# Load order, early weight conversion and early products in an attention + gated MLP + SoLU MLP kernel

## The chip, the cores and the metric

One NeuronCore of a Trainium2 chip runs the whole program. The metric is the device time of one execution in microseconds (us); lower is better. Engines are named as in the profile: PE (TensorE matmul), PEld (its weight loads), DVE (VectorE), ACT (ScalarE), POOL (GpSimd), SP (SyncE, which here only issues DMAs).

## The reference

```python
def _attn_ref(q, k, v):                    # 2 x 12 heads, 448 x 64, fp32, causal
    scores = scale * np.matmul(q, k.transpose(0, 1, 3, 2))
    scores = np.where(mask, -1000000000.0, scores)
    scores = scores - np.max(scores, axis=-1, keepdims=True)
    attn = np.exp(scores)
    attn = attn / (np.sum(attn, axis=-1, keepdims=True) + 1e-09)
    return np.matmul(attn, v)

def _moe_ref(x, w_gate, w_val, w_out):     # x 896 x 768, w_gate/w_val 768 x 1536, w_out 1536 x 768
    gate = 1.0 / (1.0 + np.exp(-(x @ w_gate)))
    return gate * (x @ w_val) @ w_out

def _moe2_ref(x, w_in, w_out, g_ln):       # w_in 768 x 1024, w_out 1024 x 768
    h = x @ w_in
    solu = h * softmax(h)
    ln = (solu - mu) / np.sqrt(var + 1e-06) * g_ln
    return ln @ w_out
```

The attention output, heads side by side, is the `x` of the first MLP, whose output is the `x` of the second. The weights arrive as 64-bit floats, given to the kernel as pairs of 32-bit words, and are turned into fp32 on the chip.

## The kernel before, in words

**Stages.** The attention works on 12 pairs of heads (`NPR`), pair 0 to 5 being batch 0 and 6 to 11 batch 1. Then come the gate/value products (L564, weight chunks 0 to 23), the product with `w_out` (L594), the product with `w_in` with the SoLU and normalisation (L626), and the last product (L687). Everything after the attention is one long row of matmuls, fed by weight chunks of 128 x 768 that pass through small rings of buffers.

**One pair of heads.** PE makes the scores (`sc_mm`, L299 and L309, tile `s`), DVE takes their row maxima (`sc_max`, L324), ACT the exponentials with their row sums (`sc_exp`, L336, tile `p`), PE transposes the exponentials in four parts u = 0 to 3 (`tr_mm`, L381, tile `t`, a ring of three PSUM buffers), which DVE (u = 0, 1; L392) and ACT (u = 2, 3; L390) copy to SBUF (tile `pt`), and PE multiplies them with v (`pv_mm`, L404, tile `x`, one PSUM buffer). The row sums go a way of their own: POOL adds a small number (`sums`, L340), DVE takes reciprocals and transposes them (`recips`, L344, L345, tile `rs32q`), SP writes them to DRAM in four small DMAs (`rs_rows`, L350, tile `rd`) and reads them back spread over 64 partitions each in two (`rs_bcast`, L356, tile `rb`). DVE then multiplies `x` by `rb` (`x_mul`, L410, tile `xf`), ACT rounds the product to the matmul type (`x_hi`, L414), and POOL subtracts that from it (`x_lo`, L419): `xy` holds a high and a low part, and each product is three matmuls. POOL also scales q (`prep_q`, L226) when `load_qk` (L218, 448 KB a pair, a ring of three) has brought it; `load_v` (L223, 256 KB) brings v.

**What sets the order.** The program has a manual schedule: each engine executes in the order in which the code issues to it, and a wait holds up all that stands behind it on that engine. `STEPS` lists, for each action, the step it belongs to within a pair; a pair begins every `PER` = 8 steps, so that action `s0` of pair p is issued at step 8p + s0, engine letter by engine letter within a step (E, A, D, S, P). SP is one such queue: the loads, the small writes and the reads of the reciprocals stand in one line.

**Weight chunks.** A chunk of 64-bit words is brought to a `raw` buffer (two of them), and `bits_steps` makes fp32 of it: ACT scales (L118), DVE does three bit operations (L121, L123, L126, tile `t`), and after the last one the load of the next chunk is issued (`dma_next`, L106). `chunk_hi` (ACT, L137) and `chunk_lo` (DVE, L140) make the high and low parts (tile `hl`). Chunks 0 and 1 are loaded in parts during the attention (`FIRST_RAW`, L99). Before, their conversion is issued at steps 86 to 103, that is with pairs 10 and 11 on the way, and that of chunks 2 and 3 at steps 102 to 117.

**Early products.** Of the first gate/value tile, the half of batch 0 needs only pairs 0 to 5, so its 36 matmuls (`early_tiles`, L436, tile `gv`) are dealt out among the last pairs' work, as soon as `hl` of chunks 0 and 1 is there: before, from step 96 on, up to two a step, the rest after the last step.

```python
        for s in range(PER * NPR + 26):
            steps(s, 'E')
            for _ in range(2):
                if s >= PER * NPR and left and next(early):
                    left -= 1
```

When a group of 18 is complete, ACT copies it to SBUF (tile `pre`, L441), in the place of its queue where the last matmul was issued. Two short matmuls (L181) stand between the last early product and the first one of L564.

Of the kernel before, what the change touches and what calls it, by code (L numbers as in the profile page):

```python
# [15 lines left out]
ALU = mybir.AluOpType  # L16
# [22 lines left out]
def f32(ap):  # L39
    return ap.bitcast(F32)  # L40
# [3 lines left out]
def attn_moe_moe2(ctx: ExitStack, tc: tile.TileContext, qk, v, w_gv, w_out, w_in2, w_out2, g_ln, out):  # L44
# [3 lines left out]
    nc = tc.nc  # L48
# [84 lines left out]
        for _ in bits_steps(it):  # L133
            pass

    def w_hi(it, hi):
        nc.scalar.copy(out=hi, in_=t_t[it])  # L137

    def w_lo(it, hi, lo):
        nc.vector.tensor_tensor(out=lo, in0=t_t.pop(it), in1=f32(hi), op=ALU.subtract)  # L140

    def chunk_hi(c):
        if c < NCH and c not in hl_t:
            hl_t[c] = ring.tile([128, 2, CH], FR, tag="hl", name="hl")
# [55 lines left out]
    with ExitStack() as actx:  # L200
# [242 lines left out]

        NPR = NH // 2
        PER = 8
        FIRST_RAW = {34: (0, 0, 1), 42: (0, 1, 2), 50: (0, 2, 3), 58: (0, 3, 4),
                     66: (1, 0, 1), 74: (1, 1, 3), 82: (1, 3, 4)}
        early = early_tiles()
        left = NE * 6 * NK

        STEPS = (
            (0, 'E', lambda p: sc_mm(p, (0, 1)), 3), (2, 'E', lambda p: sc_mm(p, (1,)), 2, 3),
            *((9 + 2 * u, 'E', lambda p, u=u: tr_mm(p, u), int(u < 2)) for u in range(4)),
            (17, 'E', lambda p: pv_mm(p, 0, 1)), (18, 'E', lambda p: pv_mm(p, 3, 2)),
            (16, 'A', lambda p: tr_copy(p, 3, 'A')),
            (1, 'A', lambda p: sc_exp(p, (3,)), 2), (2, 'A', lambda p: sc_exp(p, (0,)), 2),
            (5, 'A', lambda p: sc_exp(p, (2,)), 1), (6, 'A', lambda p: sc_exp(p, (1,)), 1),
            (23, 'A', x_hi), (15, 'A', lambda p: tr_copy(p, 2, 'A')),
            (8, 'D', recips), (-1, 'D', lambda p: sc_max(p, 3, 0), 2, 3), (0, 'D', lambda p: sc_max(p, 3, 0), 3),
            (2, 'D', lambda p: sc_max(p, 2), 2), (3, 'D', lambda p: sc_max(p, 1), 2),  # L460
            (12, 'D', lambda p: tr_copy(p, 0, 'D'), 1), (21, 'D', x_mul), (14, 'D', lambda p: tr_copy(p, 1, 'D'), 1),
            (7, 'P', sums, 1), (-8, 'P', prep_q, 3), (24, 'P', x_lo),
            (8, 'S', rs_rows), (8, 'S', rs_bcast), (-2, 'S', lambda p: load_qk(p + 2), 1), (11, 'S', lambda p: load_v(p + 2)),
        )

        sc_mm(0, (0, 1))
# [28 lines left out]
                    f(p)  # L495


        for s in range(PER * NPR + 26):
            steps(s, 'E')
            for _ in range(2):  # L500
                if s >= PER * NPR and left and next(early):
                    left -= 1
            steps(s, 'A')
            steps(s, 'D')
            steps(s, 'S')
            steps(s, 'P')
# [3 lines left out]
            for c in range(2 * NE + 2):  # L510
                e = s - 86 - 8 * c
                if e in (3, 5, 7):
                    next(bits_now)
                if e == 8 and c < 2 * NE:
                    chunk_hi(c)
                if e == 9 and c < 2 * NE:
                    chunk_lo(c)
                if e == 0:
                    bits_now = bits_steps(c)
                    next(bits_now)  # L520
# [237 lines left out]
```

## Time and profile before

| | |
|---|---|
| median of 3 runs | 488.84 us (486.95 to 490.61) |
| the profiled execution | 489.1 us, of which its span is 487.3 |
| PE busy | 476.5 us (98%), 2727 matmuls |
| DVE / ACT / POOL busy | 305.1 / 207.6 / 72.0 us |
| mean granted TensorE clock | 0.993 |
| DMA | 55.56 MB, mean 114 GB/s |

Busy times come from one profiled execution. Its time is that of the whole execution; the span runs from its first to its last instruction, and the 1.8 us between them are not in the trace. Matmuls are pipelined, so the duration of one overlaps the next; what a row of them costs is read from the chain of waits, where each piece is counted once. All times in the sections below are counted from the start of the span.

### The profile page before, as it was taken

The page shows a single profiled execution, that of the slowest core. Times are in us where ns is not written, and L with a number is a line of the kernel's source. Part 1 is how long each engine was busy: PE and PEld are TensorE (multiplying, and loading weights), DVE is VectorE, ACT ScalarE, POOL GpSimd, SP SyncE. Part 2 cuts the span into 40 slices and gives each one's busy share as a digit, 9 for nine tenths or more (in the row PEclk, how much of TensorE's full clock was granted, in tenths as well). Part 3 has the DMA queues.
Part 4 walks back from the last instruction along what each step waited for, and adds up shares of the span by engine and source line. Part 5 has one row for each costly group of instructions (what it writes and reads, how often), then busy time and mean ns, then how long its engine had stood idle before and what let it go on. Part 6 is the DMA issues. An engine that isn't in the chain of part 4 may idle for free.

```text
span 487.3 us, 7096 instructions
## 1 busy us (share of the span) xinstructions
PE 476.5 (98%) x2727; PEld 412.7 (85%) x2727; DVE 305.1 (63%) x472; ACT 207.6 (43%) x441; POOL 72.0 (15%) x121
## 2 busy tenths in 40 slices
PE   9999987899999999999999999999999999999997
PEld 7666654579999999999999999999988888899997
DVE  5676666765676777887777666777726978811110
ACT  4787768453235345345344233243321524232111
POOL 2222212110000000000000000000151778510000
PEclk9999999799999999999999999999999999999999
DMA  5245353342234335454335225444322130001001
GB/s 195 81 159 164 124 189 132 134 164 65 82 114 150 112 126 174 139 164 147 118 124 195 90 84 172 136 164 142 119 108 66 65 101 30 1 32 66 32 34 65
DMA packets 16401, 55.56 MB, mean 114 GB/s; under 512 B 2800, under 2 KB 5616, under 8 KB 16368
## 3 DMA queue, kind: packets, MB, share of 16 engines
q1 hardware_dynamic: 16368, 55.11, 33.7%
q8 instruction: 21, 0.34, 0.3%
q14 instruction: 12, 0.10, 0.1%
HBM read 52.30 MB, written 2.80 MB: 113 GB/s over the span
## 4 chain that ended last, share of the span: by engine, by line
PE 87%; DMA 5%; SPq 3%; DVE 2%; ACT 1%; issue 1%; POOL 0%; DVEq 0%; ACTq 0%; POOLq 0%
PE gv L564 34%; PE pm L594 18%; PE po L687 12%; PE h L626 12%; DMA rd<-rs32q 3%; PE x L404 2%; PE gv L436 2%; PE s L309 2%; PE t L381 2%; DMA rb<-rd 1%; PE tp L669 1%; ACT p L336 1%; SPq L350 1%; DVE sum L324 1%; SPq L356 1%
## 5 line engine op out<-in xcount | busy, mean ns | idle before, releaser
L564 PE MATMUL gv<-xy,hl 128*128 128x448 f32 x828 | 168.1, 365 | 0.0
L564 PEld LDWEIGHTS gv<-xy,hl 128*128 128x128 f32 x828 | 155.4, 188 | 12.3
L594 PE MATMUL pm<-g,hl 128*128 128x448 f32 x432 | 87.7, 365 | 0.0
L594 PEld LDWEIGHTS pm<-g,hl 128*128 128x128 f32 x432 | 81.1, 188 | 6.4
L687 PE MATMUL po<-wo,lt 128*128 128x384 f32 x336 | 60.7, 340 | 0.0
L140 DVE TENSOR_TENSOR hl<-t,hl 128x768 fp32r<-128x768 f32 x36 | 34.5, 958 | 40.9 <-ACT hl L137 39.2
L626 PE MATMUL h<-wi,xy 128*128 128x512 f32 x252 | 59.3, 396 | 0.0
L687 PEld LDWEIGHTS po<-wo,lt 128*128 128x128 f32 x336 | 58.7, 188 | 0.2 <-POOL wo L616 0.2
L626 PEld LDWEIGHTS h<-wi,xy 128*128 128x128 f32 x252 | 47.1, 188 | 11.4
L123 DVE SCALAR_TENSOR_TENSOR t<-raw,t 128x768 int32<-128x768 int32 (+1 forms) x56 | 54.3, 969 | 1.9
L118 ACT ACTIVATE raw<-raw 128x768 f32<-128x768 f32 (+1 forms) x56 | 48.0, 866 | 9.9 <-DMA raw<-in_wo_dram 6.1
L126 DVE SCALAR_TENSOR_TENSOR t<-raw,t 128x768 int32<-128x768 int32 (+1 forms) x56 | 51.2, 913 | 1.6
L336 ACT ACTIVATE p<-s,sum 128x320 f32<-128x320 f32 (+3 forms) x92 | 42.2, 484 | 10.1 <-DVE sum L324 8.1
L611 POOL TENSOR_SCALAR t<-t,g_sb 128x768 f32<-128x768 f32 x8 | 9.0, 1121 | 247.9 <-PE pm L594 247.9
L137 ACT CAST hl<-t 128x768 fp32r<-128x768 f32 x36 | 30.0, 832 | 11.9 <-DVE t L126 7.7
L121 DVE TENSOR_SCALAR t<-raw 128x768 int32<-128x768 int32 (+1 forms) x56 | 31.2, 557 | 2.8 <-ACT raw L118 2.8
L177 DVE TENSOR_TENSOR lt<-tp,lt 128x512 fp32r<-128x512 f32 x14 | 9.7, 690 | 36.4 <-ACT lt L176 36.4
L404 PE MATMUL x<-pt,vr 128*64 128x384 f32 (+3 forms) x168 | 30.5, 425 | 0.0
L189 ACT ACTIVATE wk<-gv 128x448 f32<-128x448 f32 x23 | 11.3, 542 | 44.2 <-PE gv L564 44.2
L324 DVE TENSOR_REDUCE sum<-s 128x2 f32<-128x640 f32 (+3 forms) x44 | 27.4, 677 | 3.5 <-PE s L309 3.5
L309 PE MATMUL s<-qkr,qs 64*128 64x448 f32 (+3 forms) x192 | 28.0, 416 | 0.0
L381 PE MATMUL t<-ident,p 128*128 128x128 f32 x180 | 25.3, 279 | 1.3 <-DVE pt L392 0.9
(90 smaller groups left out, 388.6 us busy)
## 6 DMA issues: line engine op xcount, KB each, us to landing
raw<-in_gv_dram SPq DMA_DIRECT2D x22, 768.0 KB
raw<-in_wo_dram SPq DMA_DIRECT2D x20, 768.0 KB
raw<-in_wi_dram SPq DMA_DIRECT2D x12, 512.0 KB
qkr<-in_qk_dram SPq DMA_DIRECT2D x11, 448.0 KB
vr<-in_v_dram SPq DMA_DIRECT2D x12, 256.0 KB
rb<-rd SPq DMA_DIRECT2D x24, 112.0 KB
out_dram<-o SPq DMA_DIRECT2D x6, 384.0 KB
raw<-in_gv_dram SPq DMA_DIRECT2D x6, 192.0 KB
```

The source lines that it names most:

```text
L118: nc.scalar.activation(out=w1.bitcast(F32), in_=w1.bitcast(F32), func=AF.Copy, scale=2.0 ** -112)
L123: nc.vector.scalar_tensor_tensor(out=tt, in0=w1, scalar=-2 ** 31, in1=tt, op0=ALU.bitwise_and, op1=ALU.bitwise_or)
L126: nc.vector.scalar_tensor_tensor(out=tt, in0=w0, scalar=29, in1=tt, op0=ALU.logical_shift_right, op1=ALU.bitwise_or)
L140: nc.vector.tensor_tensor(out=lo, in0=t_t.pop(it), in1=f32(hi), op=ALU.subtract)
L309: nc.tensor.matmul(out=ps_sc[p, i][1 - e], lhsT=q_sc[p % 2][rows, n - D:n + D], rhs=k[rows, S - n:] if e else k[rows, :n], start=False, st ...
L336: nc.scalar.activation(out=p_t[p % 2][:, POFF[i] + (1 - e) * n:POFF[i] + (2 - e) * n], in_=ps_sc[p, i][1 - e], func=AF.Exp, bias=mx, scale ...
L381: nc.tensor.transpose(ps[:, max(c, 0):max(c, 0) + 128], p_t[p % 2][:, k:k + 128], ident if c >= 0 else identx)
L404: nc.tensor.matmul(out=ps_pv[pr][d, q0:], lhsT=v_raw[pr % 3][:, (j - 1) % NQ, d], rhs=pt_t[pr][:, u, c0:c0 + S - q0], start=(j == 0), stop ...
L564: nc.tensor.matmul(out=ps[i, b], lhsT=w[:, a, cs], rhs=xy[kk][:, x, b * S:(b + 1) * S], start=(kk == 0 and a == 0 and x == 0), stop=(kk == ...
L594: nc.tensor.matmul(out=ps[b], lhsT=w[:, a, cs], rhs=g_t[kk][:, x, b * S:(b + 1) * S], start=(kk == 0 and a == 0 and x == 0), stop=(kk == N ...
L626: nc.tensor.matmul(out=h[:, n * 512:(n + 1) * 512], lhsT=xy[kk][:, a, tk], rhs=wi[n * NK + kk][:, c], start=(kk == 0 and i == 0), stop=(kk ...
L687: nc.tensor.matmul(out=ps[n], lhsT=lts[k // 4][:, a, k % 4], rhs=wo[k][:, c, cs], start=(k == 0 and i == 0), stop=(k == NF2 - 1 and i == 2))
```

## The change

The change has four parts.

**SP's order.** `load_qk(p + 2)` is issued at step 8p instead of 8p - 2, and `rs_bcast` at step 8p + 10 instead of 8p + 8. With `FIRST_RAW` at steps 9, 17, ... 65 (eight quarters of 192 KB, instead of seven loads at steps 34 to 82), the loads of q and k and of a quarter chunk now stand between the writes and the reads of one pair's reciprocals.

**Conversion of chunks 0 and 1.** Its steps are issued by a table (`FIRST_BITS`): chunk 0 at steps 64 (ACT), 68 (two DVE steps) and 76 (the third, and the load of chunk 2), chunk 1 at 72, 76 and 84 (and the load of chunk 3). The high and low parts are made by POOL instead of ACT and DVE, at steps 77 and 79, 85 and 87. Chunks 2 and 3 follow at steps 96 to 109.

**Early products.** `EARLY` deals 2, 3, 3, 3 and 10 of them at steps 96, 97, 99, 101 and 103; the other 15 follow after the last step. The first two blocks of pair 10's `pv_mm` are issued at step 98 instead of 97, beside the other two.

**Pair 0.** Its copies u = 2 and u = 3 of the transposed exponentials go from ACT to DVE.

```diff
-    def w_hi(it, hi):
-        nc.scalar.copy(out=hi, in_=t_t[it])
+    def w_hi(it, hi, eng='A'):
+        if eng == 'A':
+            nc.scalar.copy(out=hi, in_=t_t[it])
+        else:
+            nc.gpsimd.tensor_scalar(out=hi, in0=t_t[it], scalar1=1.0, scalar2=1.0, op0=ALU.mult, op1=ALU.mult)
...
+    def w_lo(it, hi, lo, eng=nc.vector):
+        eng.tensor_tensor(out=lo, in0=t_t.pop(it), in1=f32(hi), op=ALU.subtract)
...
-        FIRST_RAW = {34: (0, 0, 1), 42: (0, 1, 2), 50: (0, 2, 3), 58: (0, 3, 4),
-                     66: (1, 0, 1), 74: (1, 1, 3), 82: (1, 3, 4)}
+        FIRST_RAW = {9 + 8 * n: (n // 4, n % 4, n % 4 + 1) for n in range(8)}
+        FIRST_BITS = {64: (0,), 68: (0, 0), 76: (0, 1), 72: (1,), 84: (1, 1),
...
+        FIRST_HI, FIRST_LO = {77: 0, 85: 1}, {79: 0, 87: 1}
+        EARLY = {96: 2, 97: 3, 99: 3, 101: 3, 103: 10}
...
-            (17, 'E', lambda p: pv_mm(p, 0, 1)), (18, 'E', lambda p: pv_mm(p, 3, 2)),
-            (16, 'A', lambda p: tr_copy(p, 3, 'A')),
+            (17, 'E', lambda p: pv_mm(p, 0, 1), 0, NPR - 2), (18, 'E', lambda p: pv_mm(p, 0, 1), NPR - 2, NPR - 1),
+            (17, 'E', lambda p: pv_mm(p, 0, 1), NPR - 1), (18, 'E', lambda p: pv_mm(p, 3, 2)),
+            (16, 'A', lambda p: tr_copy(p, 3, 'A'), 1), (16, 'D', lambda p: tr_copy(p, 3, 'D'), 0, 1),
...
-            (8, 'S', rs_rows), (8, 'S', rs_bcast), (-2, 'S', lambda p: load_qk(p + 2), 1), (11, 'S', lambda p: load_v(p + 2)),
+            (8, 'S', rs_rows), (0, 'S', lambda p: load_qk(p + 2), 1), (10, 'S', rs_bcast), (11, 'S', lambda p: load_v(p + 2)),
```

On SP, around the reciprocals of pair 4, the queue before reads so (`rd` is the writes, `rb` the reads, `qkr` and `vr` the loads of a later pair, `raw` a part of a chunk):

```order
L350 DMA rd_641<-rs32q0_149 8x32 x4
L356 DMA rb_646<-rd_641 64x448 x2
L99 DMA raw_579<-in_gv_dram 128x384
L223 DMA vr0_112<-in_v_dram 128x512
L218 DMA qkr_691<-in_qk_dram 128x896
```

In the changed kernel the same pair's stretch is this:

```order
L353 DMA rd_642<-rs32q0_149 8x32 x4
L221 DMA qkr_647<-in_qk_dram 128x896
L99 DMA raw_662<-in_gv_dram 128x384
L359 DMA rb_671<-rd_642 64x448 x2
L226 DMA vr0_112<-in_v_dram 128x512
```

The load of q and k, which stood last and served pair 8, now stands behind the writes and serves pair 7; the part of a chunk has come in front of the reads too.

On PE, from pair 10's last transposes on (`p_154` belongs to pair 11, `vr_113` to pair 10, `gv` are the early products), the queue before is:

```order
L381 MATMUL t<-ident,p_153 128x128 x12
L436 MATMUL gv<-xy_76,hl 128x448 x2
L381 MATMUL t<-identx,p_154 128x128
L381 MATMUL t<-ident,p_154 128x128 x3
L404 MATMUL x<-pt,vr_113 128x448
L404 MATMUL x<-pt,vr_113 64x384 x2
L436 MATMUL gv<-xy_76,hl 128x448
L436 MATMUL gv<-xy_77,hl 128x448
L404 MATMUL x<-pt,vr_113 64x128 x2
L404 MATMUL x<-pt,vr_113 64x256 x2
```

and after the change:

```order
L384 MATMUL t<-ident,p_153 128x128 x12
L439 MATMUL gv<-xy_76,hl 128x448 x2
L384 MATMUL t<-identx,p_154 128x128
L384 MATMUL t<-ident,p_154 128x128 x3
L439 MATMUL gv<-xy_76,hl 128x448
L439 MATMUL gv<-xy_77,hl 128x448 x2
L407 MATMUL x<-pt,vr_113 128x448
L407 MATMUL x<-pt,vr_113 64x384 x2
L407 MATMUL x<-pt,vr_113 64x128 x2
L407 MATMUL x<-pt,vr_113 64x256 x2
```

The same two early products still stand first; three more have come in front of pair 10's product with v, which is now one block.

On POOL, from `x_lo` of pair 6 on (`qs` is `prep_q`, `rs8i` is `sums`, `xy` is `x_lo`), the queue before is:

```order
L419 TENSOR_TENSOR xy_76<-xf,xy_76 128x448
L340 TENSOR_SCALAR rs8i_146<-sum_142 128x8
L226 TENSOR_SCALAR qs_111<-qkr 128x448
L419 TENSOR_TENSOR xy_77<-xf,xy_77 128x448
L340 TENSOR_SCALAR rs8i_145<-sum_143 128x8
L419 TENSOR_TENSOR xy_78<-xf,xy_78 128x448
```

and after the change:

```order
L422 TENSOR_TENSOR xy_76<-xf,xy_76 128x448
L140 TENSOR_SCALAR hl<-t 128x768
L343 TENSOR_SCALAR rs8i_146<-sum_142 128x8
L143 TENSOR_TENSOR hl<-t,hl 128x768
L229 TENSOR_SCALAR qs_111<-qkr 128x448
L422 TENSOR_TENSOR xy_77<-xf,xy_77 128x448
L140 TENSOR_SCALAR hl<-t 128x768
L343 TENSOR_SCALAR rs8i_145<-sum_143 128x8
L143 TENSOR_TENSOR hl<-t,hl 128x768
L422 TENSOR_TENSOR xy_78<-xf,xy_78 128x448
```

The high part of each chunk stands in front of a pair's sums, and the low part of chunk 0 in front of the last `prep_q`.

## Rows read from the trace of the kernel before

**Rows 1.** Busy time by stretch; columns: stretch, length, engines, PEclk, DMA share, GB/s.
```profile
37.00:45.00 8.00, 8.00 (x68) 4.96 (x70) 6.05 (x14) 6.44 (x23) 2.31 (x4) 1.00 0.46 144
...
85.00:93.00 8.00, 6.21 (x22) 3.12 (x22) 5.50 (x9) 3.07 (x5) 1.42 (x1) 0.57 0.33 129
...
0.00:104.20 104.20, 96.69 (x822) 63.99 (x823) 69.03 (x139) 70.06 (x238) 24.59 (x48) 0.97 0.43 143
104.20:272.00 167.80, 167.80 (x829) 155.49 (x829) 120.33 (x168) 70.75 (x109) 0.00 (x0) 1.00 0.41 134
```

**Rows 2.** Waits to 105 us: who waited for whom, total, times, longest.
```profile
DVE xf L410 <- DMA rb<-rd: 18.1, 8, 3.4
...
SPq L356 <- DMA rd<-rs32q: 33.2, 15, 3.4
```

**Rows 3.** Timeline of SP's queue: start, duration, line, what is issued.
```profile
14.67 1.33 SPq L350 DMA_DIRECT2D rd<-rs32q  x4
17.00 1.13 SPq L356 DMA_DIRECT2D rb<-rd  x2
...
62.20 1.34 SPq L350 DMA_DIRECT2D rd<-rs32q  x4
66.67 1.09 SPq L356 DMA_DIRECT2D rb<-rd  x2
67.80 0.59 SPq L99 DMA_DIRECT2D raw<-in_gv_dram  x1
...
68.91 0.42 SPq L218 DMA_DIRECT2D qkr<-in_qk_dram  x1
69.38 1.34 SPq L350 DMA_DIRECT2D rd<-rs32q  x4
```

**Rows 4.** Timeline of PE: start, duration; in brackets the idle time ahead and its releaser.
```profile
21.61 0.26 PE L299 MATMUL s<-mk_r,mk_l 64*128 64x64 bf16 x6
...
24.36 2.36 PE L404 MATMUL x<-pt,vr 128*128 128x448 f32 x14
...
50.38 2.36 PE L404 MATMUL x<-pt,vr 128*128 128x448 f32 x14
...
79.30 2.36 PE L404 MATMUL x<-pt,vr 128*128 128x448 f32 x14
...
83.40 0.66 PE L381 MATMUL t<-ident,p 128*128 128x128 f32 x4 [0.71 <-DVE pt L392]
86.79 1.11 PE L436 MATMUL gv<-xy,hl 128*128 128x448 f32 x2 [2.73 <-ACT hl L137]
```

**Rows 5.** Chain that ended last, in order of time: start, duration, what.
```profile
44.51 2.82 DMA rb<-rd
...
65.13 2.20 PE x L404 x14
67.33 1.48 PE t L381 x12
...
95.62 0.81 PE gv L436 x4
```

**Rows 6.** Timeline of DVE, columns as in rows 4.
```profile
35.04 0.20 DVE L344 RECIPROCAL rs32t<-rs8i 128x8 f32<-128x8 f32 x1 [0.19 <-POOL rs8i L340]
...
47.45 0.62 DVE L410 TENSOR_TENSOR xf<-x,rb 128x448 f32<-128x448 f32 x1 [2.00 <-DMA rb<-rd]
```

**Rows 7.** Costliest groups: line, operation, tiles, count, busy us, mean ns.
```profile
L123 DVE SCALAR_TENSOR_TENSOR t<-raw,t 128x768 int32<-128x768 int32 (+1 forms) x56 | 54.3, 969 | 1.9
```

**Rows 8.** Timeline of POOL, columns as in rows 4.
```profile
73.29 0.56 POOL L226 TENSOR_SCALAR qs<-qkr 128x448 f32<-128x448 f32 x1 [3.06 <-DMA qkr<-in_qk_dram]
```

**Rows 9.** Lines 612 and 616: durations in ns, smallest, median, largest.
```profile
L612 POOL TENSOR_SCALAR wo<-t x8: 832/925/1424, 352.3 to 421.3; 128x768 fp32r<-128x768 f32 x8
L616 POOL TENSOR_TENSOR wo<-t,wo x8: 1840/2440/2462, 353.9 to 422.2; 128x768 fp32r<-128x768 f32 x8
```

**Rows 10.** Timeline of ACT, columns as in rows 4.
```profile
97.72 0.53 ACT L441 COPY pre<-gv 128x448 f32<-128x448 f32 x1 [0.21 <-PE gv L436]
```

More of the change, by code (lines that the diff above doesn't have):

```diff
@@ L134, in bits, with chunk_hi, chunk_lo @@
             pass
-    def w_hi(it, hi):
-        nc.scalar.copy(out=hi, in_=t_t[it])
-    def w_lo(it, hi, lo):
-        nc.vector.tensor_tensor(out=lo, in0=t_t.pop(it), in1=f32(hi), op=ALU.subtract)
-    def chunk_hi(c):
+    def w_hi(it, hi, eng='A'):
[5 more added lines that the diff above has]
+        eng.tensor_tensor(out=lo, in0=t_t.pop(it), in1=f32(hi), op=ALU.subtract)
+    def chunk_hi(c, eng='A'):
         if c < NCH and c not in hl_t:
             hl_t[c] = ring.tile([128, 2, CH], FR, tag="hl", name="hl")
-            w_hi(c, hl_t[c][:, 0])
-    def chunk_lo(c):
+            w_hi(c, hl_t[c][:, 0], eng)
+    def chunk_lo(c, eng=nc.vector):
         if c in t_t:
-            w_lo(c, hl_t[c][:, 0], hl_t[c][:, 1])
+            w_lo(c, hl_t[c][:, 0], hl_t[c][:, 1], eng)
     wi = {}
@@ L445, in attn_moe_moe2 @@
         PER = 8
-        FIRST_RAW = {34: (0, 0, 1), 42: (0, 1, 2), 50: (0, 2, 3), 58: (0, 3, 4),
-                     66: (1, 0, 1), 74: (1, 1, 3), 82: (1, 3, 4)}
+        FIRST_RAW = {9 + 8 * n: (n // 4, n % 4, n % 4 + 1) for n in range(8)}
+        FIRST_BITS = {64: (0,), 68: (0, 0), 76: (0, 1), 72: (1,), 84: (1, 1),
+                      96: (2,), 97: (2,), 99: (2,), 101: (2,), 104: (3,), 105: (3,), 107: (3,), 109: (3,)}
+        FIRST_HI, FIRST_LO = {77: 0, 85: 1}, {79: 0, 87: 1}
+        EARLY = {96: 2, 97: 3, 99: 3, 101: 3, 103: 10}
         early = early_tiles()
@@ L453, in attn_moe_moe2 @@
             *((9 + 2 * u, 'E', lambda p, u=u: tr_mm(p, u), int(u < 2)) for u in range(4)),
[L454 to L455 removed]
+            (17, 'E', lambda p: pv_mm(p, 0, 1), 0, NPR - 2), (18, 'E', lambda p: pv_mm(p, 0, 1), NPR - 2, NPR - 1),
+            (17, 'E', lambda p: pv_mm(p, 0, 1), NPR - 1), (18, 'E', lambda p: pv_mm(p, 3, 2)),
+            (16, 'A', lambda p: tr_copy(p, 3, 'A'), 1), (16, 'D', lambda p: tr_copy(p, 3, 'D'), 0, 1),
             (1, 'A', lambda p: sc_exp(p, (3,)), 2), (2, 'A', lambda p: sc_exp(p, (0,)), 2),
             (5, 'A', lambda p: sc_exp(p, (2,)), 1), (6, 'A', lambda p: sc_exp(p, (1,)), 1),
[L458 removed]
+            (23, 'A', x_hi), (15, 'A', lambda p: tr_copy(p, 2, 'A'), 1), (14, 'D', lambda p: tr_copy(p, 2, 'D'), 0, 1),
             (8, 'D', recips), (-1, 'D', lambda p: sc_max(p, 3, 0), 2, 3), (0, 'D', lambda p: sc_max(p, 3, 0), 3),
@@ L495, in steps @@
                     f(p)
+        bits_now = {}
         for s in range(PER * NPR + 26):
             steps(s, 'E')
-            for _ in range(2):
-                if s >= PER * NPR and left and next(early):
-                    left -= 1
+            for _ in range(EARLY.get(s, 0)):
+                left -= next(early)
             steps(s, 'A')
@@ L508, in attn_moe_moe2 @@
                 dma_part(*FIRST_RAW[s])
[L510 to L520, printed above, removed]
+            for c in FIRST_BITS.get(s, ()):
+                if c not in bits_now:
+                    bits_now[c] = bits_steps(c)
+                next(bits_now[c])
+            if s in FIRST_HI:
+                chunk_hi(FIRST_HI[s], 'P')
+            if s in FIRST_LO:
+                chunk_lo(FIRST_LO[s], nc.gpsimd)
         while left:
```

## The prediction

> **What bounds the kernel now.** I read the busy time by stretch first [rows 1]. From 104.2 us on PE is busy for all of 167.8 us at full clock, and what it is fed with comes no later than before (chunks 2 and 3 are converted some steps earlier); so only the first 104.2 us, the attention, can give or lose time. In there PE is busy for 96.7 us, but that flatters: from 85 to 93 us the mean granted clock is 0.57, so most of that stretch ran at 1.2 instead of 2.4 GHz.
>
> The waits say who is late [rows 2]. SP waits 33.2 us in 15 places for the reciprocals' writes to land before it may read them back, and DVE waits 18.1 us in 8 places for these reads. SP's queue shows why [rows 3]: writes at 62.20, done issuing at 63.54, reads only at 66.67, that is 3.13 us with the queue standing, and only then the loads. One turn is 69.38 - 62.20 = 7.18 us.
>
> PE's own timeline gives the comparison [rows 4]. The product with v of pair 1 starts at 24.36 and that of pair 5 at 50.38: (50.38 - 24.36) / 4 = 6.505 us a pair, with PE full in the stretch from 37 to 45 [rows 1]. From pair 6 on SP's 7.18 us rule: pair 9 starts at 79.30 instead of 24.36 + 8 x 6.505 = 76.40. Then two stalls end the stage badly: 0.71 us for a copy on DVE (ahead of 83.40), where conversion work stands in front of it, and 2.73 us for the high part of chunk 0 (ahead of 86.79), after which the clock falls.
>
> **The change part by part.**
>
> *SP's order.* A turn now issues 1.34 (writes) + 0.42 (q and k) + 0.59 (quarter chunk) inside the wait. The reads go out when the writes have landed: 1.00 us after their issue at the shortest (pair 0: 14.67 + 1.33 to 17.00), 3.13 at the longest [rows 3], so 2.4 to 4.5 us into the turn. Add 1.09 for the reads and 0.5 for v (the gap from 68.39 to 68.91): 4.0 to 6.1 us. Both ends lie under 6.505, so SP stops being the bound and PE's pitch should hold to pair 9: 2.9 us gained.
>
> What is late next is the way of one reciprocal. From `recips` to `x_mul` before: 0.5 (reciprocal and transpose) + 1.34 + 3.13 + 3.3 (the reads: 0.5 for the first issue, 2.82 to landing [rows 5]) = 8.3 us. Allowed are 47.45 - 2.00 - 35.04 = 10.4 us before DVE has to wait at all [rows 6]. New is that 640 KB stand ahead of the reads. At the stretch's mean of 143 GB/s [rows 1] these take 4.5 us, and they are issued 2 us before the reads, so up to 2.5 us are added; at the other end 2.1 are saved, since the writes no longer follow a load of q and k and may land after 1.0 instead of 3.13. Even the bad end, 10.8, is over by only 0.4 us. I take nothing, since the shift is mostly of who waits in front of whom.
>
> The Trainium skill ("DMA: Bandwidth & Descriptors", section "Queues, rings and completion order") says that each DMA engine consumes its descriptors in ring order, which speaks against this part: what is issued ahead of the reads is also moved ahead of them. The trace agrees as far as it goes, the writes landing 1.00 us after issue with no load close ahead of them and 3.13 behind one [rows 3]. Strictly applied the rule gives the bad end above, with 0.4 us of wait a pair.
>
> *q and k later.* For pair 3 the load used to go out early; now it follows pair 0's writes, at about 16.0. A load of q and k takes 73.29 - 68.91 = 4.4 us to its use [rows 3, 8], then 0.56 for `prep_q`: 21.0, and PE starts pair 3's scores at 21.61 [rows 4]. It is covered by 0.6 us; without that cover it costs the excess, once. For pair 7: 35.04 + 0.5 + 1.34 + 4.4 + 0.56 = 41.8 against 21.61 + 4 x 6.505 = 47.6, so later pairs have 5.8 us to spare.
>
> *Conversions.* Eight steps are 6.505 us, and step 25 is at 24.36, so a step number is a time. DVE gets two steps of at most 0.97 us [rows 7] in each of three pairs, up to 1.94 us. In a pair at full pitch it is idle 1.95 of 8 us [rows 1], or 1.6 a pair: over by 0.3 at most, in a copy that PE needs only for the next pair. I count 0.3 once; bounds 0 and 0.9. ACT gets one scaling in two pairs, under 1 us against 1.56 of 8 us idle: nothing. POOL, busy 2.31 of 8 us, gets for each chunk 0.93 + 2.44 us [rows 9]. Chunk 0: low part from step 79 (68.3) to 70.7, then `prep_q` of pair 11 to 71.3, needed at 21.61 + 8 x 6.505 = 73.65. Chunk 1: last DVE step issued at 72.3, its end by 74.2, high part 75.1, low part behind `sums` by 78; PE asks for it at 80.1. Both are in time, so the 2.73 us stall goes, and with it what made the clock fall. The 0.71 us stall goes too, since no conversion stands in front of that copy any more.
>
> The Trainium skill ("SBUF — State Buffer", section "Who interferes with whom") says that a DVE instruction with two SBUF inputs and a GpSimd instruction that reads SBUF exclude each other for a whole instruction. Such are DVE's last two conversion steps and POOL's low parts. Rows 9 show 1.84 to 2.46 us for the same operation, which agrees without proving it. By the rule a conversion step could be held for up to 2.44 us; that is rival C's way in.
>
> *The end of the stage.* Before: pair 10's transposes end at 83.40 + 0.66 = 84.06, and the next stage starts at 104.20: 20.14 us. After: they end at 76.40 + 2.20 + 1.48 = 80.08 [rows 5], 3.98 earlier. What is left for PE is 36 early products at 0.81 / 4 (7.29), 16 transposes at 1.48 / 12 (1.97) and two products with v at 2.20 (4.40): 13.66 us. Dealing them out differently adds no work. I add 1.2 us of stalls: 0.3 from DVE above, 0.2 at pair 11's first transposes, whose exponentials come just in time, and 0.7 because the copy `pre`, 0.53 us [rows 10], now stands on ACT ahead of a rounding and the two copies that pair 11's product needs: three of some 0.5 us each less the 0.9 that PE still has to do. Bounds of this sum: 0 and 2.5. So 14.9 instead of 20.14: 5.3 us gained.
>
> *Pair 0's copies* move about 1 us from ACT to DVE, which waits for PE there; nothing.
>
> Sum: 4.0 + 5.3 = 9.3 us off the profiled execution's 489.1, or 479.8. The median of the runs, 488.84, is 0.3 lower, so I say 479.6.
>
> **The rivals.**
>
> B. The pairs do not reach PE's pitch, since the reads land late behind the loads or DVE runs out of time: half of SP's excess stays, (7.18 - 6.505) / 2 x 8 = 2.7 us. For it: DVE waits for the reads in eight pairs. Against: the 2.1 us to spare. 482.3 us.
>
> C. The conversions come late (POOL and DVE in each other's way, or `sums` and `prep_q` waiting behind the low part), PE stands as long as before and the clock falls again. Only the 4.0 us stay: 484.8. For it: the low part is one of POOL's longest instructions, and 2 us are all that is to spare. Against: both chunks start over 10 us earlier.
>
> D. Slower. `x_mul` of pair p stands on DVE ahead of the reciprocals of pair p + 2, so a way of L us forces a pitch of (L + 1.14) / 2, where 1.14 is `x_mul` (0.62, [rows 6]) and the copy behind it (some 0.5). The stage ends at 24.36 + 8 x pitch + 3.68 + 14.9, which is 104.2 at a pitch of 7.66: it decides from L = 14.2 us, 5.9 above the old 8.3. At L = 15.5 (pitch 8.3) the result is 494. For it: 640 KB are put ahead of the reads. Against: the bad end gives only 10.8.
>
> E. The order of loads makes no difference and the end pays back in new stalls what it gains: 488.
>
> **How the numbers follow.** Forecast 0.68, B 0.12, C 0.12, D 0.05, E 0.03. A measurement of this kernel tells about 1% (4.9 us) from no change. The forecast and B are faster than that, 0.80; C and E lie within it, 0.15; D is slower, 0.05. The forecast's own range is 478 to 482: no stalls at the lower end, the bounds of the stalls at the upper. The low end 477.5 also takes in half a microsecond of spread; the high end 486 takes in B and C, and leaves out D and E.
>
> **What would show it.** Right: SP's wait between writes and reads filled with two loads, starts of the product with v 6.5 us apart up to pair 9, no wait of PE at the first early product, full clock throughout the attention, and L564 starting near 95 us. Wrong: `x_mul` waiting over 2 us for the reads in most pairs (B, D), PE waiting for POOL's `hl` or a clock near 0.5 after 80 us (C), `prep_q` of pair 3 holding PE at 21.6, or PE idle for more than 2.5 us between 80 and 95.

## The result, and the profile after

Four executions of the changed kernel took 479.64 us (median; 479.04 to 480.31), four of the kernel before, run beside them, 488.01 us. The ratio is 0.9845, with an interval of 0.9805 to 0.9886: faster by 1.1 to 2.0%, where 479.6 us were forecast. Measured twice more, the changed kernel took 484.48 and 484.07 us; the last part of the experiments is about that. The profiled execution took 479.04 us with a span of 477.2, both some 10.1 us less than before.

The time by stretch of the changed kernel (stretch, length, engines, PEclk, DMA share, GB/s) answers to [rows 1]:

```profile
76.00:84.00 8.00, 8.00 (x57) 5.32 (x56) 5.24 (x11) 5.45 (x20) 2.06 (x3) 1.00 0.22 78
84.00:92.00 8.00, 7.29 (x42) 5.23 (x41) 3.60 (x7) 2.79 (x5) 1.14 (x1) 1.00 0.34 117
0.00:94.23 94.23, 91.91 (x822) 62.41 (x823) 68.31 (x140) 67.05 (x234) 29.78 (x52) 1.00 0.53 165
94.23:262.00 167.77, 167.77 (x829) 155.46 (x829) 118.92 (x166) 70.83 (x109) 0.00 (x0) 1.00 0.39 130
```

The attention is 9.97 us shorter, and the stretch that ran at a mean granted clock of 0.57 is gone: every stretch shows 1.00, the level of 2.4 GHz. In this execution nothing has changed from the long row on. PE's busy time in the attention fell by 4.8 us although it does the same 822 matmuls; 3.2 of that (17.41 against 14.20) lie behind pair 10's transposes, where the clock had fallen.

The waits to 105 us of the changed kernel (who, for whom, total, times, longest) answer to [rows 2]:

```profile
SPq L353 <- DVE rs32q L348: 20.7, 8, 10.3
SPq L359 <- DMA rd<-rs32q: 10.0, 10, 2.5
DVE xf L413 <- DMA rb<-rd: 1.6, 2, 0.9
PE gv L439 <- ACT pre L444: 0.7, 1, 0.7
```

DVE waited 18.1 us for the reads of the reciprocals and now waits 1.6. SP waited 33.2 us for the writes to land and now waits 10.0; instead it waits 20.7 us for DVE to make the next reciprocals, that is, SP has time left over. Of PE's waits only the last row is new.

SP's timeline of the changed kernel, in mid attention and around the first whole chunk (`raw` at 65.35, 768 KB), answers to [rows 3]:

```profile
45.38 0.33 SPq L226 DMA_DIRECT2D vr<-in_v_dram  x1
47.63 1.30 SPq L353 DMA_DIRECT2D rd<-rs32q  x4
49.03 0.36 SPq L221 DMA_DIRECT2D qkr<-in_qk_dram  x1
49.43 0.43 SPq L99 DMA_DIRECT2D raw<-in_gv_dram  x1
50.03 1.09 SPq L359 DMA_DIRECT2D rb<-rd  x2
...
54.14 1.31 SPq L353 DMA_DIRECT2D rd<-rs32q  x4
...
65.35 0.37 SPq L106 DMA_DIRECT2D raw<-in_gv_dram  x1
67.14 1.30 SPq L353 DMA_DIRECT2D rd<-rs32q  x4
71.07 1.09 SPq L359 DMA_DIRECT2D rb<-rd  x2
```

A turn is 54.14 - 47.63 = 6.51 us, PE's own pitch. The writes are issued by 48.93 and the reads go out at 50.03, 1.10 us later, with both loads issued in between; the last load ahead of these writes (`vr` at 45.38) lies 2.25 us back. Where a load of a whole chunk was issued 1.8 us ahead of the writes, the reads followed them by 71.07 - 68.44 = 2.63 us.

PE's timeline of the changed kernel (start, duration; in brackets the idle time ahead and its releaser) answers to [rows 4], and one row of the kernel before, its first matmul of the long row, is set under it:

```profile
23.46 2.36 PE L407 MATMUL x<-pt,vr 128*128 128x448 f32 x14
...
75.49 2.36 PE L407 MATMUL x<-pt,vr 128*128 128x448 f32 x14
77.79 1.53 PE L384 MATMUL t<-ident,p 128*128 128x128 f32 x12
79.07 0.65 PE L439 MATMUL gv<-xy,hl 128*128 128x448 f32 x2
...
87.79 0.85 PE L439 MATMUL gv<-xy,hl 128*128 128x448 f32 x3 [0.71 <-ACT pre L444]
...
94.06 10.18 PE L568 MATMUL gv<-xy,hl 128*128 128x448 f32 x49
```

```profile
104.03 6.33 PE L564 MATMUL gv<-xy,hl 128*128 128x448 f32 x30
```

These rows give the measure used below, the time **to the row**: from the start of pair 1's product with v to the start of the long row. It is 104.03 - 24.36 = 79.67 us before and 94.06 - 23.46 = 70.60 after, 9.07 less. (Pair 1's product itself starts between 23.5 and 24.5 us in the profiled executions of this study, with no relation to the edit, so what lies ahead of it is left out. Pair 0's copies, the fourth part of the change, were not run alone; with them on DVE pair 1's product starts at 23.46 to 24.46, with them on ACT at 24.07 to 24.36, which shows neither gain nor loss.) Pair 9 starts 75.49 - 23.46 = 52.03 us after pair 1, 6.504 a pair, where before it took 54.94. No wait stands ahead of the first early product any more; one of 0.71 us stands ahead of product 19.

POOL's timeline of the changed kernel answers to [rows 8]:

```profile
18.66 0.57 POOL L229 TENSOR_SCALAR qs<-qkr 128x448 f32<-128x448 f32 x1 [3.53 <-DMA qkr<-in_qk_dram]
...
65.02 1.09 POOL L140 TENSOR_SCALAR hl<-t 128x768 fp32r<-128x768 f32 x1 [3.14 <-DVE t L126]
...
66.70 1.81 POOL L143 TENSOR_TENSOR hl<-t,hl 128x768 fp32r<-128x768 f32 x1
...
73.76 1.81 POOL L143 TENSOR_TENSOR hl<-t,hl 128x768 fp32r<-128x768 f32 x1
```

Chunk 0 is ready by 68.51 us, 10.6 us before PE asks for it at 79.07. Chunk 1 is ready by 75.57; the first 18 early products use chunk 0 alone, so PE asks for chunk 1 only with product 19, at 87.79.

So the forecast and the first measurement agree to 0.04 us. The experiments ask whether they do so for the reasons given.

### The profile page after: what moved, and what is told of

It is laid out like the page before. It is cut to its first block, busy times and chain, and to the rows that moved or that the text cites. A ratio compares the mean times of both kernels' runs of the same rounds, so it can differ in the third digit from the quotient of the medians.

```text
span 477.2 us, 7091 instructions
## 1 busy us (share of the span) xinstructions
PE 471.7 (99%) x2727; PEld 411.1 (86%) x2727; DVE 303.0 (63%) x472; ACT 204.8 (43%) x437; POOL 77.2 (16%) x125
## 4 chain that ended last, share of the span: by engine, by line
PE 98%; DVE 1%; ACT 1%; issue 0%; ACTq 0%
PE gv L568 35%; PE pm L598 18%; PE po L691 12%; PE h L630 12%; PE x L407 5%; PE s L312 5%; PE t L384 5%; PE gv L439 2%; PE tp L673 1%; PE warm L274 1%; PE s L302 1%; ACT p L339 0%; DVE sum L327 0%; PE t L274 0%; DVE pt L395 0%
## 5 line engine op out<-in xcount | busy, mean ns | idle before, releaser
L143 DVE TENSOR_TENSOR hl<-t,hl 128x768 fp32r<-128x768 f32 x34 | 32.6, 959 | 40.3 <-ACT hl L138 38.6
L123 DVE SCALAR_TENSOR_TENSOR t<-raw,t 128x768 int32<-128x768 int32 (+1 forms) x56 | 52.6, 940 | 1.9
L126 DVE SCALAR_TENSOR_TENSOR t<-raw,t 128x768 int32<-128x768 int32 (+1 forms) x56 | 51.2, 914 | 1.6
L339 ACT ACTIVATE p<-s,sum 128x320 f32<-128x320 f32 (+3 forms) x92 | 42.2, 484 | 12.3 <-DVE sum L327 10.6
L138 ACT CAST hl<-t 128x768 fp32r<-128x768 f32 x34 | 28.4, 835 | 4.2 <-PE pm L598 4.2
L407 PE MATMUL x<-pt,vr 128*64 128x384 f32 (+3 forms) x168 | 28.6, 410 | 0.0
L312 PE MATMUL s<-qkr,qs 64*128 64x448 f32 (+3 forms) x192 | 27.0, 405 | 0.0
L138 ACT CAST wi<-t 128x512 fp32r<-128x512 f32 x12 | 7.5, 622 | 42.7 <-DVE t L126 42.7
```

The costliest lines, as they stand in the source:

```text
L123: nc.vector.scalar_tensor_tensor(out=tt, in0=w1, scalar=-2 ** 31, in1=tt, op0=ALU.bitwise_and, op1=ALU.bitwise_or)
L126: nc.vector.scalar_tensor_tensor(out=tt, in0=w0, scalar=29, in1=tt, op0=ALU.logical_shift_right, op1=ALU.bitwise_or)
L143: eng.tensor_tensor(out=lo, in0=t_t.pop(it), in1=f32(hi), op=ALU.subtract)
L312: nc.tensor.matmul(out=ps_sc[p, i][1 - e], lhsT=q_sc[p % 2][rows, n - D:n + D], rhs=k[rows, S - n:] if e else k[rows, :n], start=False, st ...
L339: nc.scalar.activation(out=p_t[p % 2][:, POFF[i] + (1 - e) * n:POFF[i] + (2 - e) * n], in_=ps_sc[p, i][1 - e], func=AF.Exp, bias=mx, scale ...
L407: nc.tensor.matmul(out=ps_pv[pr][d, q0:], lhsT=v_raw[pr % 3][:, (j - 1) % NQ, d], rhs=pt_t[pr][:, u, c0:c0 + S - q0], start=(j == 0), stop ...
```

## The experiments

The theory was that of the prediction: the new order of the loads gives 4.0 us, and the early conversion on POOL the rest, by taking away the wait of 2.73 us and the fall of the clock behind it. The rival was that both come from the loads alone.

### The loads alone

**Both edits of the loads, nothing else** (`e1_loads_only`), made from the kernel before:

```diff
-        FIRST_RAW = {34: (0, 0, 1), 42: (0, 1, 2), 50: (0, 2, 3), 58: (0, 3, 4),
-                     66: (1, 0, 1), 74: (1, 1, 3), 82: (1, 3, 4)}
+        FIRST_RAW = {9 + 8 * n: (n // 4, n % 4, n % 4 + 1) for n in range(8)}
...
-            (8, 'S', rs_rows), (8, 'S', rs_bcast), (-2, 'S', lambda p: load_qk(p + 2), 1), (11, 'S', lambda p: load_v(p + 2)),
+            (8, 'S', rs_rows), (0, 'S', lambda p: load_qk(p + 2), 1), (10, 'S', rs_bcast), (11, 'S', lambda p: load_v(p + 2)),
```

> The kernel before with the new order of SP alone (loads between the writes and the reads, chunk quarters from step 9). My theory: two separate gains; this one ends SP's rule, so the products with v of pairs 1 and 9 start 52.0 us apart instead of 54.9, while the stalls behind pair 9 stay (PE waits some 2.7 us at the first early product and the clock falls to 0.5): 2.9 us off, about 485.1 against 488.0. Rival (the order of loads is hidden anyway, all of the gain is in the conversions): 54.9 us apart and 488. Rival (the whole gain hangs on it): 480.

It took 481.51 us, ratio 0.991 (0.9891 to 0.993; the kernel before took 486.37 in this comparison, with executions from 483.94 to 490.27). Its PE timeline, and below that its time by stretch:

```profile
24.27 2.36 PE L404 MATMUL x<-pt,vr 128*128 128x448 f32 x14
...
76.31 2.36 PE L404 MATMUL x<-pt,vr 128*128 128x448 f32 x14
81.54 0.67 PE L436 MATMUL gv<-xy,hl 128*128 128x448 f32 x2 [1.41 <-ACT hl L137]
...
96.29 3.89 PE L563 MATMUL gv<-xy,hl 128*128 128x448 f32 x18
```

```profile
80.00:88.00 8.00, 6.59 (x40) 4.26 (x39) 7.34 (x11) 3.94 (x8) 1.95 (x2) 1.00 0.39 117
```

To the row it is 96.29 - 24.27 = 72.02 us: the loads alone bring 7.65 of the 9.07 us. The pitch was as expected (76.31 - 24.27 = 52.04), but behind it 4.75 us are gained too, where the theory had the old end of the stage unchanged. Pair 10's transposes end at 80.13 here, and behind them 16.32 us are left where 20.14 stood before. The wait for the high part is 1.41 us instead of 2.73, and PE's busy time in that stretch is 14.91 us instead of 17.41, with the clock at 1.00 throughout: 1.32 us of wait and 2.50 us at the lower clock are saved there, 3.82 in all.

Why the wait is shorter is read on DVE. In the kernel before, the chain that ended last around the third conversion step of chunk 0 (start, duration, what), and the row of DVE's timeline for the `x_mul` in it:

```profile
80.88 3.38 DMA rb<-rd
84.38 0.62 DVE xf L410
85.01 0.87 DVE t L126
85.90 0.84 ACT hl L137
86.79 1.11 PE gv L436 x2
```

```profile
84.38 0.62 DVE L410 TENSOR_TENSOR xf<-x,rb 128x448 f32<-128x448 f32 x1 [1.04 <-DMA rb<-rd]
```

And DVE's timeline of the kernel with the new loads:

```profile
79.14 0.61 DVE L410 TENSOR_TENSOR xf<-x,rb 128x448 f32<-128x448 f32 x1
79.67 0.95 DVE L126 SCALAR_TENSOR_TENSOR t<-raw,t 128x768 int32<-128x768 int32 x1
```

Before, the step stands behind an `x_mul` that waited for the late reads, and the high part and PE's first early product follow right behind it. With the new loads the `x_mul` waits no more, with the same step behind it. PE's wait for `hl` was in part SP's delay, passed on by DVE's queue; the 1.41 us that are left are there without any wait for reads.

**Only q and k and the reads** (`e8_qk_only`): the second hunk above without the first, so that the parts of the chunks are loaded as before.

> The kernel before with only the load of q and k between the writes and the reads of the reciprocals; the parts of the chunks stay behind the reads and at their old steps. My theory: what counts is that the writes no longer stand behind a load of q and k and that the queue does not idle; a turn is 1.34 + up to 3.13 + 1.09 + 0.59 + 0.5, at most 6.65 and mostly less: pairs 1 to 9 take 52.0 us and the time is that of the first run, 481.5. Rival (both loads must stand in the wait): 53 us or more, 483 to 486.

It took 480.86 us, ratio 0.9852 (0.9823 to 0.9882). Its product of pair 1 starts at 24.07, of pair 9 at 76.10 and the row at 96.09: to the row 72.02 us, the same as with both edits. Moving the load of q and k from ahead of the writes to behind them is enough; the earlier quarters of the chunks add nothing to it.

The fall of the clock is not in every execution of the kernel before. Of the 41 that were run beside the experiments, 5 show a mean granted clock of 0.999 or 1.000 and took 485.12 us (median; 483.94 to 486.34), the other 36 show 0.989 to 0.997 and took 487.60 (484.84 to 490.27). All eight executions of the two kernels with only the loads changed show 0.999 or 1.000.

### The conversions and the engine that does them

**The changed kernel with the old order of the loads** (`e2_old_load_order`):

```diff
-            (8, 'S', rs_rows), (0, 'S', lambda p: load_qk(p + 2), 1), (10, 'S', rs_bcast), (11, 'S', lambda p: load_v(p + 2)),
+            (8, 'S', rs_rows), (8, 'S', rs_bcast), (-2, 'S', lambda p: load_qk(p + 2), 1), (11, 'S', lambda p: load_v(p + 2)),
```

> The changed kernel with SP's old order of writes, reads and loads of q and k; all else as changed. My theory: SP's turn is about 7.2 us again, pairs 1 to 9 take 54.9 us instead of 52.0, and no stall at the end: 2.9 us more than the changed kernel, about 482.5. Rival (conversions alone): 479.6. Rival (the whole gain hangs on the order): 488.

It took 495.55 us, ratio 1.0204 (1.0175 to 1.0233): slower than the kernel before, where 482.5 was expected. SP's, ACT's and PE's timelines and the time by stretch of this kernel:

```profile
67.85 0.59 SPq L99 DMA_DIRECT2D raw<-in_gv_dram  x1
```

```profile
71.24 0.88 ACT L118 ACTIVATE raw<-raw 128x768 f32<-128x768 f32 x1 [5.49 <-DMA raw<-in_gv_dram]
```

```profile
73.99 0.34 PE L302 MATMUL s<-mk_r,mk_l 64*128 64x64 bf16 x6 [4.83 <-ACT p L339]
...
85.98 2.36 PE L407 MATMUL x<-pt,vr 128*128 128x448 f32 x14
...
104.55 1.69 PE L568 MATMUL gv<-xy,hl 128*128 128x448 f32 x7
```

```profile
70.00:80.00 10.00, 6.01 (x36) 4.04 (x35) 4.85 (x10) 8.01 (x29) 3.90 (x5) 0.66 0.58 204
```

The last quarter of chunk 1 is issued at 67.85, behind the reads of its turn; ACT's scaling, now issued early, stands in front of a pair's exponentials and waits 5.49 us for it; PE waits 4.83 us for these, and the clock falls. To the row it is 104.55 - 23.57 = 80.98 us, 1.31 more than before. Another 5.0 us, with which the two profiled executions differ (494.54 against 489.1), lie in the long row (the last part of this section). The 1.31 are the sum of two large pieces. Pair 9's product starts at 85.98, 62.41 us after pair 1's, which is 7.47 more than before; from there to the row it takes 18.57 us, 6.16 less than before (104.03 - 79.30 = 24.73) and the same as in the changed kernel (94.06 - 75.49 = 18.57). So the early conversion does clear the end of the stage even with the old order of the loads, but it costs more than that ahead of it, in PE's wait of 4.83 us and the lower clock behind it. And the parts don't add up: the loads alone bring 7.65 us, the other parts alone lose 1.31, and all together bring 9.07.

**Early conversion on ACT and DVE** (`e3_convert_act_dve`):

```diff
-                chunk_hi(FIRST_HI[s], 'P')
+                chunk_hi(FIRST_HI[s])
...
-                chunk_lo(FIRST_LO[s], nc.gpsimd)
+                chunk_lo(FIRST_LO[s])
```

> The changed kernel with the high and low parts of chunks 0 and 1 on ACT and DVE at the same early steps, instead of on POOL. My theory: the time at which they are done counts, not the engine; DVE gets 0.96 us more in two pairs, over its idle share by up to 1 us each: 479.6 to 481. Rival (POOL as the engine is what makes it work, DVE runs out of time and PE stands): 483 or more, with PE waiting over 2 us for copies on DVE.

It took 485.96 us, ratio 0.9989 (0.9963 to 1.0015), but little of that is the engine's doing. To the row it is 95.91 - 24.21 = 71.70 us, 1.10 more than in the changed kernel, with two waits of PE for exponentials (0.48 and 0.29 us) that the changed kernel doesn't have there. The time of 479.6 to 481 that was expected is missed by some 5 us, and these come in the long row. The last kernel below gives the price of the engine without that.

### The early products

**Dealt out as before** (`e4_deal_as_before`):

```diff
-        EARLY = {96: 2, 97: 3, 99: 3, 101: 3, 103: 10}
+        EARLY = {s: 2 for s in range(PER * NPR, PER * NPR + 18)}
...
-            (17, 'E', lambda p: pv_mm(p, 0, 1), 0, NPR - 2), (18, 'E', lambda p: pv_mm(p, 0, 1), NPR - 2, NPR - 1),
-            (17, 'E', lambda p: pv_mm(p, 0, 1), NPR - 1), (18, 'E', lambda p: pv_mm(p, 3, 2)),
+            (17, 'E', lambda p: pv_mm(p, 0, 1)), (18, 'E', lambda p: pv_mm(p, 3, 2)),
```

> The changed kernel with the early products dealt out as before (two a step from step 96) and the first blocks of pair 10's product with v at their old step. My theory: dealing adds and removes no work, the gain at the end comes from the conversions: 479.6, within 0.8 either way, and PE's wait of 0.71 us for the copy of the first group (pre) may go, since that copy then lies beside pair 11's product. Rival (the new dealing is what keeps PE from standing): 2 us or more slower, PE waiting for ACT's copies at pair 10's product.

479.26 us, ratio 0.9865 (0.9847 to 0.9882); to the row 94.56 - 24.22 = 70.34 us. The new dealing is worth nothing, or costs 0.26: it pays the wait of 0.71 us for `pre`, which isn't there with the old one, and has 0.44 us less of PE's busy time behind pair 10's transposes (14.20 against 14.64).

**That wait taken away** (`e7_pre_later`), from the changed kernel: each group of 18 gets a PSUM tile of its own, and the first copy is issued behind ACT's copies of pair 11.

```diff
-        pre = {}
+        pre, pre_now = {}, []
...
-                both = ps_s.tile([128, 2, 512], F32, tag="s", name="gv")
                 for i in range(2):
-                    ps = both[:, i, :S]
+                    ps = ps_s.tile([128, 2, 512], F32, tag="s", name="gv")[:, 0, :S]
...
-                    nc.scalar.copy(out=pre[t, i], in_=ps)
+                    if i:
+                        nc.scalar.copy(out=pre[t, i], in_=ps)
+                    else:
+                        pre_now.append((pre[t, i], ps))
...
             steps(s, 'A')
+            while s >= PER * NPR + 8 and pre_now:
+                o, i_ = pre_now.pop()
+                nc.scalar.copy(out=o, in_=i_)
```

> The changed kernel with a PSUM tile of its own for each group of 18 early products, and the copy of the first group behind ACT's copies for pair 11 instead of ahead of them. My theory: PE's wait of 0.71 us goes and none takes its place: 0.5 to 0.7 us less, 479.0. Rival (the wait only moves to pair 11's product with v): the same time as the changed kernel. If the long row falls to 206.7 ns a matmul, 5 us more, and the attention alone tells.

478.56 us (478.16 to 478.86), ratio 0.9803 (0.9777 to 0.9829), the fastest of all. PE waits for no `pre`; to the row 93.90 - 24.23 = 69.67 us, 0.93 less. Product 19 had waited because it belongs to the second group, which shared its tile with the first, then being copied. The edit does two things at once, so which of the two would have been enough is open.

### The changed kernel again, and the pace of the long row

**The changed kernel, unaltered** (`a0_changed_again`), measured again.

> The changed kernel itself, on the chip of the runs beside it, for their comparison: 479.6, the first product of the long row 70.6 us after pair 1's product with v.

484.48 us (483.75 to 484.97, six executions), ratio 0.9925 (0.99 to 0.9949): the same kernel, 4.84 us slower than in the first measurement. To the row it is 94.34 - 23.74 = 70.60 us, not a hundredth more. The chain of waits of the first measurement's profile, and then of this one (start, duration):

```profile
94.23 167.89 PE gv L568 x828
262.11 87.56 PE pm L598 x432
349.67 0.14 PE h L184 x2
349.81 50.48 PE h L630 x216
```

```profile
94.50 171.20 PE gv L568 x828
265.70 89.28 PE pm L598 x432
354.98 0.14 PE h L184 x2
355.12 50.47 PE h L630 x216
```

The same 828 and 432 matmuls take 3.31 and 1.72 us longer, 5.03 together, without a wait and at a granted clock of 1.00. One takes 167.89 / 828 = 202.8 ns or 171.20 / 828 = 206.8 ns; behind the next two short matmuls (L184) both are alike again. It is the same in single instructions; line 568 of the first and of this profile (smallest, median and largest duration in ns):

```profile
L568 PE MATMUL gv<-xy,hl x828: 362/365/450, 94.1 to 261.8; 128*128 128x448 f32 x166
```

```profile
L568 PE MATMUL gv<-xy,hl x828: 367/369/448, 94.3 to 265.3; 128*128 128x448 f32 x166
```

So the row has two paces. The slower one was also that of the kernels above with the old order of the loads and with conversion on ACT and DVE (171.20 us in both).

In the single starts of the trace, the quicker pace is a pattern of steps, about 199, 207, 203 and 203 ns with a fifth of 203 now and then; the slower one is 206 or 207 nearly every time, never under 205. The early products ahead of the row, the same form of matmul, go at the quicker pace in either case. Between them and the row stand only the two short matmuls (128 x 64), so the theory became that these tip it, by their place in the pattern. The ten traces of this study with two of them bear it out: in the seven at the quicker pace (the kernel before among them) two steps lie between the last long step (205 to 207 ns) and the first short matmul, as in 207, 202, 203; in the three at the slower pace (the second measurement, the old order of the loads, and ACT and DVE) it is one, as in 207, 202.

**Three short matmuls instead of two** (`e5_step_off_three`), from the kernel with ACT and DVE:

```diff
-        for _ in range(2):
+        for _ in range(3):
             nc.tensor.matmul(out=ps[:, :D], lhsT=l, rhs=r, start=True, stop=True)
```

> The run with the conversion on ACT and DVE, with three short matmuls instead of two ahead of the long row (and ahead of the w_in row). In that run the long row went at 206.7 ns a matmul instead of 202.8, all at full granted clock. My theory: the pace is settled by the moment at which the long row sets in, not by ACT and DVE, so another number of short matmuls can bring 202.8 back: 481.0 instead of 486.0. Rival (the engines that convert slow the row down, through SBUF or otherwise): 206.7 stays, 486.

486.1 us, ratio 0.9961 (0.9945 to 0.9977), the row at 171.19 us: missed. A third one doesn't set it right. Here too one step lies ahead of the short ones, so the run doesn't decide on the place.

**The changed kernel a third time** (`a1_changed_third`), on another chip.

> The changed kernel a third time, as control. It has been measured at 479.6 with its long row at 202.8 ns a matmul, and at 484.5 with the row at 206.7, with the same 70.6 us in the attention both times. My theory: either value, all executions of one job alike; nothing between.

One execution, the profiled one, took 479.92 us, with a row of 167.89; the other five took 483.93 to 484.61. So it isn't the chip, and not one pace a comparison either. Of the changed kernel's 16 executions in the study 5 lie at 479.0 to 480.3 and 11 at 483.8 to 485.0, with none between.

**Without the two short matmuls ahead of the row** (`v0_no_step_off`). They write where the row's first matmul begins afresh, so nothing of the result is left out.

```diff
-                if c == 0:
-                    step_off(ps[i, bs[0]], w[:, 0, :128], xy[0][:, 0, :D])
```

> The changed kernel without the two short matmuls ahead of the long row (their product is overwritten, so nothing of the result is left out). In the slow runs the 15 early products ahead of the two short ones still went at 202.6 ns on average, and the row behind them at 206.7. My theory: the two short matmuls are where the pace is lost; without them the row carries on at 202.8 whatever the job: 479.4. Rival (the pace belongs to the long row or to the chip): 206.7 and 484.3 if the control is slow, 479.4 if it is fast.

479.47 us (478.67 to 479.59, five executions), ratio 0.9831 (0.9809 to 0.9853). Its chain has the row at the quicker pace:

```profile
94.85 167.81 PE gv L566 x828
```

**The same with `pre` later** (`v7_pre_later_no_step_off`): this edit and that of the kernel with `pre` later.

> The version with the later copy of the first group of early products, without the two short matmuls too. My theory: 478.6, the sum of both. Rival (without the short matmuls the row sets in at 206.7): 483.5.

478.63 us (478.10 to 478.91), ratio 0.9817 (0.9795 to 0.9838); to the row 93.56 - 24.04 = 69.52 us, the row 167.81. It is no faster than with the short matmuls, which there met the quicker pace in all six executions.

**The same with conversion on ACT and DVE** (`v3_act_dve_no_step_off`): this edit and that of the kernel with ACT and DVE.

> The run with the conversion on ACT and DVE, without the two short matmuls ahead of the long row. That kernel was slow twice, on two chips, with two short matmuls and with three. My theory: 202.8 ns a matmul, so 480.8, and what is left over the changed kernel, 1.1 us, is the price of ACT and DVE. Rival (the engines that convert make the row slow): 486.

480.45 us (480.07 to 481.13), ratio 0.9853 (0.9824 to 0.9881), and the row, 171.20 with the short matmuls, is down to 167.81, so the engines that convert don't make the row slow. All 14 executions without the short matmuls lie where the quicker pace puts them. Against 479.47 with POOL the difference is 1.0 us; to the row it is 96.03 - 24.46 = 71.57 us against 94.69 - 23.89 = 70.80, 0.8 us, though in the trace with POOL one turn of reciprocals was late (below) and cost PE some 0.3 us. So POOL saves about 1 us.

## Why the prediction was right, and where it was not

**The sum was right.** It had 4.0 + 5.3 = 9.3 us; the trace shows 9.07 to the row. Pair 10's transposes end at 79.32, which is 3.84 us earlier if both are counted from pair 1's product (84.06 - 24.36 against 79.32 - 23.46), and what is left behind them takes 94.23 - 79.32 = 14.91 us, where 14.9 was predicted and 20.14 stood before: 5.23 us gained. That the two terms come out so closely is in part luck.

**SP's order** went as worked out: 2.91 us by pair 9 where 2.9 was taken. The reads go out 50.03 - 47.63 = 2.40 us into the turn, the lower end of 2.4 to 4.5, so that rivals B and D never came near. (The longest landing of the writes was read as 3.13 us, but [rows 2] have a wait of 3.4; nothing hangs on it.)

**The way of one reciprocal** was taken at nothing; DVE waits 1.6 us for it, in two places, and PE for neither. Both lie ahead of 27 us, in pairs 0 and 1; the bad end, 0.4 us a pair behind 640 KB of loads, is not seen. The Trainium skill ("DMA: Bandwidth & Descriptors", section "Queues, rings and completion order") has each engine consume its descriptors in ring order. The runs agree on the side of the writes: 1.10 us with the last load 2.25 us ahead of them, 2.63 behind a whole chunk, and 4.99 behind one in the trace without the two short matmuls (67.56 + 1.30 to 73.85). On the side of the reads no wait of `x_mul` shows a cost in mid attention, with 640 KB issued within the 1.0 us ahead of them; how long these reads took to land is not read there. In that late turn of the other trace the reads took 4.51 us to land, where 2.82 and 3.38 were seen in the kernel before.

**q and k of pair 3** are scaled at 18.66 us, after 3.53 us of POOL's waiting; with 0.57 for the scaling that is 19.23, where 21.0 was reckoned, and PE doesn't wait.

**The step that failed is "Conversions",** in its last part: "so the 2.73 us stall goes, and with it what made the clock fall". Both are gone, but the credit was wrong. The order of the loads alone halves that wait and keeps the clock at 1.00. The 5.3 us at the end of the stage were booked as the work of the early conversion; of the 5.23 that were measured, the loads alone bring 20.14 - 16.32 = 3.82, and the early conversion with the new dealing adds 72.02 - 70.60 = 1.42 to the row. The stall of 0.71 us ahead of the last transposes, too, is gone with the loads alone, with the conversions at their old steps. Rival C was priced by the same mistake: without the conversions in time there remain not 4.0 us but 7.65. The prediction saw DVE's 18.1 us of waiting for the reads and used it for the pitch alone. It didn't follow DVE's queue on to the conversion step that stands behind the waiting `x_mul`, and so took one delay for two. Nor is the end the loads' alone: with the old order of the loads the early conversion cleared it as well, and lost more ahead of it. Either cure does most of the work at the end, so no sum of separate gains could show what one of them is worth. That the right sum came out is because both causes were removed together.

**The conversion on POOL** itself was sized on the safe side: 1.81 us for a low part where up to 2.44 was taken. The time to spare was misread: "PE asks for it at 80.1" was said of chunk 1, but that is chunk 0's moment, 10.6 us behind its low part, and chunk 1 is asked for at 87.79, 12.2 us behind its own. So rival C's "2 us are all that is to spare" was too small. The exclusion of DVE and GpSimd that was drawn from the Trainium skill ("SBUF — State Buffer", section "Who interferes with whom") was not put to the test: in the timelines DVE's steps with two SBUF inputs (from 58.06, 63.98, 70.49 and 71.47 us, under 1 us each) meet none of POOL's low parts.

**The stalls** were allowed 1.2 us, 0.7 of it for `pre`. PE waits 0.71 us for `pre`, but at product 19 and not at pair 11's product, and the other 0.5 is not seen. Instead the work took 14.20 us (PE's busy time) where 13.66 was reckoned, 0.14 of it for the two short matmuls, which the sum left out. Two errors of half a microsecond cancel.

**Not in the prediction at all** is the pace of the long row, "from 104.2 us on PE is busy for all of 167.8 us" and so not able to change. It can, by 5.0 us, and in 11 of 16 executions of the changed kernel it does. The forecast of 479.6 is the time at the quicker pace; 484.3 at the slower (the middle of those 11) lies within the range, 477.5 to 486, by luck and not by argument. Of the kernel before only one execution has a trace, at the quicker pace; whether its row changes too isn't known, and so the ratio above holds for the quicker pace of the changed kernel; at the slower one it was 0.9925 and, with one quick execution in six, 0.9918.

## What to carry to other kernels

A wait that ends on a busy engine's queue delays all that stands behind it there: before two terms of a sum are added, follow each delayed instruction to what its engine does next, and see whether the second wait is the first one passed on. On a queue that issues DMAs, small writes that must come back soon belong ahead of large loads, and the loads fit into the time in which the writes land. And measure a variant more than once: a row of like matmuls that nothing holds up may still change its pace, which the busy share and the clock don't show, only the mean time of one.

## What the runs showed of the hardware that was not expected

The same row of 128 x 448 matmuls, each with its weight load, at a granted clock of 1.00 and without a wait, runs at 202.8 or at 206.8 ns a matmul, and keeps its pace over 1260 of them, 255.5 or 260.5 us. The paces differ between executions of one kernel on one chip. Shown is that with two 64-column matmuls ahead of the row both paces occur, with three (one kernel) the slower, and that without them 14 executions of three kernels lie at the quicker one. The place in the pattern of steps at which the short matmuls set in goes with the pace in all ten traces with two of them, but no run set that place on purpose, so that it decides is not shown; what in the chip keeps the pace stays open. Leaving them out, together with the later copy of `pre`, gives 478.63 us, 1.0 less than the changed kernel at its quicker pace and 5.6 less than at the slower.
